# Moving four pieces of work in a fused attention and SoLU kernel: the flag's sum, one exponential, one copy, one split

## The chip, the cores and the metric

The kernel runs on one core of a Trainium2 chip. The metric is device time in microseconds (us) of one execution, the median of several runs. A core has five engines with a queue of instructions each: TensorE (PE, whose weight loads are shown as PEld), VectorE (DVE), ScalarE (ACT), GpSimd (POOL) and SyncE (SP). They run side by side and wait for each other by semaphores. Transfers are issued from the queues of SP, ACT and POOL and carried out by 16 DMA engines.

## The reference

Two stages follow each other. The first is block-sparse attention over 4 batches, 8 heads, 768 positions and 64 numbers per head; a mask of 24 by 24 blocks allows the neighbouring blocks, the first and the last row and column of blocks, and three sampled blocks for each row of blocks. The second takes the 3072 rows of 512 numbers and computes a layer with the SoLU activation and a layer norm.

```
scores = q @ k.T / sqrt(64);  scores[not mask] = -1e9
attn   = exp(scores - max) / (sum + 1e-9)
x      = (attn @ v) as rows of 8 heads x 64        # 3072 x 512
h      = x @ w_in                                  # 3072 x 1024
solu   = h * exp(h - max) / (sum + 1e-9)
ln     = (solu - mean) / sqrt(var + 1e-6) * g_ln
out    = ln @ w_out                                # 3072 x 512
```

All inputs and the output are float32 in memory; the kernel multiplies in bfloat16.

## The kernel before, in words

The work goes in 12 passes (NPASS): three for each batch, each for 256 queries (PC = 2 tiles of 128). A pass has 12 units (SLOTS): four pairs of heads (NP), three steps over the keys (UP) each. A unit is four products for the scores of two heads (`scores`, L416, tile sco, two buffers), one exponential on ScalarE over 128 x 1024 scores (`exps`, L427, tile exs), and eight products with the values (`outs`, L444, tile op). At the end of a pair DVE divides by the sums (`normalise`, L457 and L458, tile xb).

The second stage of one pass lies among the units of the next. xb is transposed to xT (by DMA, `x_turn`), `h_mms` (L487) multiplies with w_in, `e_exp` (L496) takes the exponential on ScalarE, `solu` (L508) multiplies on DVE, `ln_turn` (L513) transposes by DMA to lnT, `o_mms` (L547) multiplies with w_out, centred beforehand (w_cen), `stats` and `rstd` (L522 to L540) find the factor of the norm, `scaled` (L556, L558) applies it and `store` (L563) writes the rows.

Nothing is scheduled by a planner: `at(when, fn, ...)` puts each step at a time, counted in units, and `emit` records all steps sorted by it. What is recorded for one engine is done in that order. The changed steps are these.

- **k and q of a later batch.** They are loaded, cast by GpSimd, transposed by DMA into a tile pd and then copied by GpSimd (`shift`, shown as L327, the line of the helper `copy`) into KT and QT, since the two heads of a pair stand one below the other. For the last pair (NP - 1) q's first two of six blocks are copied ahead of k; then k whole, then q's other four.
- **e in the last pass.** In the last pass (b0 = SLOTS * LP) the layer of the pass before is squeezed into fewer units. `e_at` gives the times of e, solu and lnT of its first tile.
- **The end.** When the last attention unit is through, the last pass's own layer follows, without attention to fill the gaps. Three quarters of its xT come by DMA, the last quarter by TensorE (`x_last`, tile x_tp) and a copy on DVE (L860); `h_end` (L869) multiplies its halves, `ln_mm` and `ln_out` transpose solu over TensorE and ScalarE. In the stream of TensorE around it stand products of the layer before (o_mms of LP - 1).
- **The flag.** The kernel leaves out the maxima of both softmaxes. It therefore checks that all sums were in range: `check_r` and `check_e` write ones and zeros, `check_sum` (L930, L931) adds them up on DVE to a flag for each partition, `check_bad` (L938) adds those up with one product on TensorE, `check_out` (L941) casts it to an integer bad_i. Behind it all engines load the flag (L995) and branch (L996): only if it is not zero, a general path written as loops is run. Otherwise it is jumped over, and SP waits for all transfers (L1022).
- **The last tile's output** comes in two halves of 256 columns (`o_half`, L897, tiles oe1a and oe1b); DVE scales the first, and SP stores it (L909), ScalarE scales and stores the second (L906). The flag's product stands between the fifth and the sixth of the eight products of the second half.

Of the kernel before, what the change touches and what calls it, by code (L numbers as in the profile page):

```python
# [7 lines left out]
FP32 = mybir.dt.float32  # L8
# [200 lines left out]
def kernel(  # L209
# [11 lines left out]
    nc = tc.nc  # L221
# [13 lines left out]
    KF = d_ff // 128  # L235
# [6 lines left out]
    PC = 2  # L242
# [3 lines left out]
    NP = H // 2  # L246
# [13 lines left out]
    bad = const_pool.tile([128, 1], FP32)  # L260
    bad_i = const_pool.tile([1, 1], I32)
    ones_c = const_pool.tile([128, 1], FP32)
# [20 lines left out]
    p_sco = work.enter_context(tc.tile_pool(name="p_sco", bufs=2, space=bass.MemoryType.PSUM))  # L283
    p_op = work.enter_context(tc.tile_pool(name="p_op", bufs=1, space=bass.MemoryType.PSUM))
    p_h = work.enter_context(tc.tile_pool(name="p_h", bufs=1, space=bass.MemoryType.PSUM))
# [4 lines left out]
    def at(when, fn, *args):  # L290
        plan.append((when, len(plan), fn, args))

    def emit():
        for _, _, fn, args in sorted(plan, key=lambda x: x[:2]):
            fn(*args)
        plan.clear()
# [5 lines left out]
    def natural(b, pr, key):  # L302
        r = KR if b == 0 and key == "k" and pr else D
        if b:
            x0 = 2 * PW * pr + (PW if key == "q" else 0)
        elif key == "q":
            x0 = k_w + PW * pr
        else:
            x0 = PW + NCH * 2 * KR * (pr - 1) if pr else 0
        return nat[:, x0 : x0 + NCH * 2 * r].rearrange("p (c h r) -> p c h r", h=2, r=r)  # L310
# [84 lines left out]
    def unit(s):  # L395
        ps, r = divmod(s, SLOTS)
        pr, u = divmod(r, UP)
        b, j = divmod(ps, NPB)
        return ps, b, j, pr, u
# [174 lines left out]
    with tc.manual_schedule():  # L574
# [4 lines left out]
                          in_=bass.AP(tensor=_t32, offset=0, ap=[[2 * NR, NB], [1, 2 * NR]]))  # L579
# [59 lines left out]
        for pr in range(1, NP):  # L639
            nc.scalar.activation(  # L640
                out=natural(0, pr, "k")[:, :, :, D:KR].rearrange("p c h r -> p (c h) r"),
                in_=zer[:, 0:NB].rearrange("p (o r) -> p o r", o=1).broadcast_to(
                    [128, NCH * 2, NB]),
# [7 lines left out]
        for i, x0, x1 in ((0, 0, QW), (1, QW, S)):  # L651
            nc.tensor.matmul(m_ps[0:KR, i, 0 : x1 - x0], mask_l, sel_f[:, x0:x1],
                             start=True, stop=True)
# [4 lines left out]
        def spread(x, n):  # L658
            return x.rearrange("p (o c) -> p o c", o=1).broadcast_to([NB, n, x.shape[-1]])
# [20 lines left out]
        for h0, n, i, x0, x1 in ((0, 2, 0, 0, QW), (0, 1, 1, QW, S), (1, 1, 1, QW, S)):  # L680
            nc.scalar.copy(out=rows(QT[0], h0, h0 + n)[:, :, x0:x1],
                           in_=spread(m_ps[D:KR, i, 0 : x1 - x0], n))
# [87 lines left out]
        for s in range(n_units):  # L770
            ps, b, j, pr, u = unit(s)
# [25 lines left out]
        for b in range(1, B):  # L797
            loads, casts, turns, shifts, v_loads, v_casts = first if b == 1 else then
            t0 = SLOTS * NPB * (b - 1)
            for (key, pr), t_l, t_c in zip(kq + vs, loads + v_loads, casts + v_casts):  # L800
                at(t0 + t_l, load, nc.sync, srcs[key], b, pr, key)
                at(t0 + t_c, cast, nc.gpsimd, b, pr, key)
            for pr, t_t in enumerate(turns):
                at(t0 + t_t, turn_dma, b, pr)

            at(t0 + shifts[6] - 0.05, shift, b, NP - 1, "q", 0, PC)
            for (key, pr), t_s in zip(kq, shifts):
                at(t0 + t_s, shift, b, pr, key, PC if (key, pr) == ("q", NP - 1) else 0)


        def layer(ps, i, hs, es, os):
# [14 lines left out]
        LP = NPASS - 1  # L826
# [17 lines left out]
        for i, t0 in ((0, b0), (1, b0 + 4)):  # L844
            for when, n0, n1 in ((3.9, 0, 2), (4.85, 2, 5), (5.86, 5, 8)):
                at(t0 + when, h_mms, ps, i, n0, n1)

            e_at = (6.5, 7.0, 7.05) if i == 0 else (6.85, 6.86, 6.87)
            for when, fn in zip(e_at, (e_exp, solu, ln_turn)):
                at(t0 + when, fn, ps, i)  # L850
        at(b0 + 8.2, stats, ps, 0)
# [2 lines left out]
        def x_last():  # L854
            tp = p_op.tile([128, 1024], BF16, tag="op", name="x_tp")[:, 0 : PC * 128]
            for i in range(PC):
                nc.tensor.matmul(tp[:, i * 128 : (i + 1) * 128],
                                 xb_of[LP][:, KD - 1, i, :], ident,
                                 is_transpose=True, start=(i == 0), stop=(i == PC - 1))
            nc.vector.tensor_copy(  # L860
                out=xT_of[LP][:, (KD - 1) * PC : KD * PC, :],
                in_=tp.rearrange("p (i t) -> p i t", t=128))

# [22 lines left out]

        o2 = {}

        def o_half(half, pool, tag, c0=0, c1=KF):
            if c0:  # L890
                pass
            elif pool is p_sco:
                o2[half] = p_sco.tile([128, 2, HF], FP32, tag=tag, name="oe1a")[:, 0, 0:256]
            else:
                o2[half] = pool.tile([128, d_model], FP32, tag=tag, name="oe1b")[:, 0:256]
            for c in range(c0, c1):
                nc.tensor.matmul(o2[half], lnT_of[LP, 1][:, c, :],  # L897
                                 w_cen_sb[:, c, half * 256 : (half + 1) * 256],
                                 start=(c == 0), stop=(c == KF - 1), skip_group_check=True)
# [13 lines left out]
        def tile_in(pool, tag, name):  # L913
            if pool is p_sco:
                return lambda: p_sco.tile([128, 2, HF], FP32, tag=tag, name=name)[:, 0, :]
            return lambda: pool.tile([128, d_model], FP32, tag=tag, name=name)
# [14 lines left out]
            nc.vector.tensor_scalar(out=bad, in0=n_ok[:, 0:1], scalar1=float(n_r + n_e),  # L931
                                    scalar2=None, op0=ALU.is_lt)

        bad_ps = []

        def check_bad():
            bad_ps.append(p_h.tile([1, 1], FP32, tag="h", name="bad_ps"))
            nc.tensor.matmul(bad_ps[0], bad, ones_c, start=True, stop=True)  # L938

        def check_out():  # L940
            nc.vector.tensor_copy(out=bad_i, in_=bad_ps[0])  # L941

        end = SLOTS * NPASS
        A, V = nc.scalar, nc.vector
        for n, (fn, *args) in enumerate((
            (h_end, 0, 2, KD),
            (e_exp, LP, 0),
            (o_mms, LP - 1, 0, 5, 8),
            (scaled, LP - 1, 0, A),
            (store, LP - 1, 0),  # L950
            (stats, LP - 1, 1),
            (rstd, LP - 1, 1),
            (check_r, n_r - 2 * PC, n_r),
            (h_end, 1, 0, KD),
            (solu, LP, 0),
            (stats, LP, 0),
            (e_exp, LP, 1),
            (o_mms, LP - 1, 1, 0, 3, tile_in(p_op, "op", "o_10")),
            (ln_mm, 0),
            (ln_out, 0, A),  # L960
            (o_mms, LP - 1, 1, 3, 8),
            (solu, LP, 1),
            (rstd, LP, 0),
            (stats, LP, 1),
            (o_mms, LP, 0, 0, 2, tile_in(p_sco, "sco", "oe0")),
            (ln_mm, 1),
            (ln_out, 1, A),
            (rstd, LP, 1),
            (check_e,),
            (check_sum,),  # L970
            (o_mms, LP, 0, 2, 8),
            (scaled, LP - 1, 1, A),
            (store, LP - 1, 1),
            (scaled, LP, 0, A),
            (store, LP, 0),
            (o_half, 0, p_sco, "sco"),
            (o_half, 1, p_op, "op", 0, 5),
            (check_bad,),
            (o_half, 1, p_op, "op", 5, KF),
            (scale_half, 0, V, nc.sync),  # L980
            (check_out,),
            (scale_half, 1, A, nc.scalar),
        )):
            at(end + 0.01 * n, fn, *args)
        at(end - 5.0, x_turn, LP, 0, 2)
        at(end - 3.1, x_turn, LP, 2, KD - 1)
        at(end - 1.175, h_end, 0, 0, 2, (0,))
        at(end - 1.12, h_end, 0, 0, 2, (1,))
        at(end - 1.0, x_last)
        at(end - 1.9, check_r, 0, n_r - 2 * PC)  # L990
        at(end - 1.05, o_mms, LP - 1, 0, 0, 5)
        emit()

    work.close()
# [32 lines left out]
```

## Time and profile before

| | |
|---|---|
| time, median of 3 runs | 210.65 us (210.59 to 210.71) |
| the profiled execution | 210.66 us, of which its span is 208.9 us |
| PE busy | 198.0 us (95%) |
| ACT busy | 174.6 us (84%) |
| DVE busy | 140.3 us (67%) |
| POOL busy | 109.1 us (52%) |
| mean granted clock of TensorE | 0.991 |

The span goes from the first to the last instruction of the program; some 1.8 us lie around it. Busy times are sums over the whole span. In the timeline a row gives start, duration, engine, line, what is done, output tile and input tile with shapes and a count, and in brackets how long the engine had been idle before it and what ended that. In the waits' view a row gives who waited for whom, the sum in us, how often, and the longest. In the view of one line a row gives minimum, median and maximum in ns, and the start of the first and the last in us. In the DMA view a queue's row gives packets, MB and the packets' time as a share of the 16 engines' time in the stretch; an issue's row gives what is moved, the issuing queue, its size and the time from issue to landing.

### The profile page before, as it was taken

The page shows a single profiled execution, that of the slowest core. Times are in us where ns is not written, and L with a number is a line of the kernel's source. Part 1 is how long each engine was busy: PE and PEld are TensorE (multiplying, and loading weights), DVE is VectorE, ACT ScalarE, POOL GpSimd, SP SyncE. Part 2 cuts the span into 40 slices and gives each one's busy share as a digit, 9 for nine tenths or more (in the row PEclk, how much of TensorE's full clock was granted, in tenths as well). Part 3 has the DMA queues.
Part 4 walks back from the last instruction along what each step waited for, and adds up shares of the span by engine and source line. Part 5 has one row for each costly group of instructions (what it writes and reads, how often), then busy time and mean ns, then how long its engine had stood idle before and what let it go on. Part 6 is the DMA issues. An engine that isn't in the chain of part 4 may idle for free.

```text
span 208.9 us, 5591 instructions
## 1 busy us (share of the span) xinstructions
PE 198.0 (95%) x2204; PEld 137.9 (66%) x2238; DVE 140.3 (67%) x329; ACT 174.6 (84%) x208; POOL 109.1 (52%) x161
## 2 busy tenths in 40 slices
PE   7989999999999999999999999999999999999980
PEld 2669867676676676676666677667667667665450
DVE  5885888987656656666656656656655755768970
ACT  6898989889889889889889889888988988875750
POOL 7989698688686384377196366197450011011120
PEclk9999999999999999999999999999999999999996
DMA  5999999899999899896999899997924915635331
GB/s 159 345 364 220 369 376 275 190 199 307 154 288 277 192 252 264 201 202 169 191 323 198 195 289 236 196 284 90 250 81 89 112 54 81 163 69 84 100 123 37
DMA packets 73906, 42.02 MB, mean 201 GB/s; under 512 B 55828, under 2 KB 69396, under 8 KB 73876
## 3 DMA queue, kind: packets, MB, share of 16 engines
q1 hardware_dynamic: 72932, 40.06, 80.4%
q0 software_dynamic: 528, 1.05, 2.7%
q10 hardware_dynamic: 416, 0.52, 0.8%
q8 instruction: 18, 0.29, 0.6%
q14 instruction: 12, 0.10, 0.2%
HBM read 23.07 MB, written 6.29 MB: 141 GB/s over the span
## 4 chain that ended last, share of the span: by engine, by line
PE 81%; DMA 9%; issue 2%; POOL 2%; ACT 1%; DVE 1%; SPq 1%; POOLq 0%
PE sco L416 28%; PE o L547 17%; PE op L444 16%; PE h L487 16%; DMA st_q<-in_q_dram 3%; DMA w_out_f<-in_moe_w_out_dram 3%; DMA st_k<-in_k_dram 3%; PE he L869 1%; PE oe L547 1%; PE mean_ps L750 1%; POOL VA L327 1%; SPq L318 1%; DVE solu L508 1%; POOL nat L327 1%; ACT e L496 1%
## 5 line engine op out<-in xcount | busy, mean ns | idle before, releaser
L427 ACT ACTIVATE exs<-sco 128x1024 bf16<-128x1024 f32 x144 | 140.6, 1024 | 8.7 <-PE sco L416 6.3
L416 PE MATMUL sco<-QT,KT 88*128 88x256 bf16 x576 | 86.6, 272 | 0.8 <-ACT exs L427 0.5
L416 PEld LDWEIGHTS <-KT 88*128 88x128 bf16 x576 | 54.1, 97 | 32.4 <-issue 5.7
L444 PE MATMUL op<-VA,exs 128*128 128x65 bf16 x1152 | 51.8, 194 | 0.5
L444 PEld LDWEIGHTS <-exs 128*128 128x128 bf16 x1152 | 48.5, 97 | 3.7 <-DVE xb L458 0.3
L487 PE MATMUL h<-w_in_sb,xT 128*128 128x512 bf16 x153 | 48.6, 378 | 0.6
L547 PE MATMUL o<-w_cen_sb,lnT 128*128 128x512 bf16 x166 | 43.2, 379 | 0.5
L540 POOL TENSOR_TENSOR rstd<-vpe,mhalf 128x1 f32<-128x1 f32 x24 | 13.2, 550 | 47.8 <-DVE vpe L538 41.3
L457 DVE RECIPROCAL recip_all<-op 128x4 f32<-128x4 f32 x48 | 8.7, 182 | 41.5 <-PE op L444 41.3
L496 ACT ACTIVATE e<-h 128x1024 bf16<-128x1024 f32 x22 | 22.5, 1024 | 12.3 <-PE h L487 10.8
L522 DVE BATCH_NORM_STATS2 stats<-solu 128x6 f32<-128x512 bf16 x48 | 30.6, 679 | 0.0
L327 POOL COPY KT<-pd 64x768 bf16<-64x768 bf16 x24 | 20.1, 838 | 17.4 <-DMA pd<-nat 15.8
L508 DVE TENSOR_TENSOR solu<-h,e 128x1024 bf16<-128x1024 f32 x22 | 26.7, 1215 | 1.4 <-ACT e L496 1.3
L327 POOL COPY QT<-pd 64x768 bf16<-64x768 bf16 (+2 forms) x30 | 20.8, 694 | 10.8 <-DMA pd<-nat 9.5
L547 PEld LDWEIGHTS <-lnT 128*128 128x128 bf16 x176 | 15.9, 97 | 13.8 <-DMA lnT<-solu 0.2
L558 DVE TENSOR_SCALAR ot<-o,rstd 128x512 f32<-128x512 f32 x20 | 15.0, 750 | 10.8 <-issue 6.9
L458 DVE TENSOR_TENSOR xb<-op,recip_all 128x256 bf16<-128x256 f32 x48 | 20.4, 424 | 1.7
L487 PEld LDWEIGHTS <-xT 128*128 128x128 bf16 x176 | 16.2, 98 | 4.2 <-DMA xT<-xb 0.5
L327 POOL CAST nat<-st_q 128x768 bf16<-128x768 f32 (+2 forms) x19 | 14.0, 736 | 7.8 <-DMA st_q<-in_q_dram 7.7
L327 POOL CAST nat<-st_k 128x768 bf16<-128x768 f32 x15 | 12.7, 850 | 3.3 <-DMA st_k<-in_k_dram 3.0
L327 POOL CAST VA<-st_v 128x768 bf16<-128x768 f32 x16 | 13.4, 842 | 1.9 <-DMA st_v<-in_v_dram 1.3
L740 POOL TENSOR_SCALAR w_out_sb<-w_out_f,g_ln_sb 128x512 bf16<-128x512 f32 x8 | 5.7, 724 | 2.1 <-DMA w_out_f<-in_moe_w_out_dram 2.1
(89 smaller groups left out, 114.7 us busy)
## 6 DMA issues: line engine op xcount, KB each, us to landing
st_v<-in_v_dram SPq DMA_DIRECT2D x16, 384.0 KB, 5.2
out_dram<-ot SPq DMA_DIRECT2D x23, 256.0 KB, 2.8
st_k<-in_k_dram SPq DMA_DIRECT2D x15, 384.0 KB, 5.4
st_q<-in_q_dram SPq DMA_DIRECT2D x12, 384.0 KB, 6.9
w_out_f<-in_moe_w_out_dram SPq DMA_DIRECT2D x4, 512.0 KB, 7.5
st_q<-in_q_dram SPq DMA_DIRECT2D x4, 256.0 KB, 6.9
w_in_sb<-in_moe_w_in_dram POOLq DMA_DIRECT2D x1, 1024.0 KB, 11.5
st_q<-in_q_dram SPq DMA_DIRECT2D x4, 128.0 KB, 4.7
```

The costliest lines, as they stand in the source:

```text
L327: eng.tensor_copy(out=o, in_=i)
L416: nc.tensor.matmul(sco[:, hh, kk * QW : (kk + 1) * QW], KT[b % 2][0:KR, h * NCH + 2 * u + kk, :], QT[b % 2][0:KR, h * NCH + PC * j : h * N ...
L427: nc.scalar.activation(out=exs_of[ps, pr][:, u].rearrange("p a b c -> p (a b c)"), in_=sco_of.pop(s).rearrange("p a b -> p (a b)"), func=A ...
L444: nc.tensor.matmul(op[:, hh, ic, :], exs[:, u, hh, kk, ic * TQ : (ic + 1) * TQ], VA[b % 2][:, 2 * pr + hh, 2 * u + kk, :], start=(u == 0 a ...
L458: nc.vector.tensor_tensor(out=xb_of[ps][:, pr].rearrange("p c (h d) -> p h c d", h=2), in0=op[:, :, :, 0:D], in1=recip.broadcast_to([TQ, 2 ...
L487: nc.tensor.matmul(h_of[ps, i][:, half, :], xT_of[ps][:, c * PC + i, :], w_in_sb[:, c, half * HF : (half + 1) * HF], start=(c == 0), stop= ...
L496: nc.scalar.activation(out=o, in_=h, func=ACT.Exp, scale=1.0, accum_out=esum_all[:, t : t + 1])
L508: nc.vector.tensor_mul(out=so, in0=h, in1=e)
L522: nc.vector.bn_stats(out=stat_of[ps, i][:, half, :], in_=so[:, half, :])
L540: nc.gpsimd.tensor_tensor(out=rstd_of[ps, i], in0=vpe, in1=mhalf, op=ALU.pow)
L547: nc.tensor.matmul(ops_of[ps, i], lnT_of[ps, i][:, c, :], w_cen_sb[:, c, :], start=(c == 0), stop=(c == KF - 1), skip_group_check=True)
L558: nc.vector.tensor_scalar(out=o, in0=i_, scalar1=r, scalar2=None, op0=ALU.mult)
```

## The change

Four places are changed; the program computes the same.

- For the last pair of a later batch, k too is copied in two parts: k's first two blocks, q's first two, k's other four, q's other four.
- In the last pass, e of the first tile goes from 6.5 to 7.01 units, so that it is recorded behind the exponential at 7 and not ahead of it.
- The last quarter of x is transposed behind three of the five products of o that preceded it, and its copy to xT goes from DVE to ScalarE.
- The flag's sum on DVE goes behind the scaling of the last tile's first half, its product on TensorE behind the second half's eight products, and its cast follows.

```diff
-            at(t0 + shifts[6] - 0.05, shift, b, NP - 1, "q", 0, PC)
             for (key, pr), t_s in zip(kq, shifts):
-                at(t0 + t_s, shift, b, pr, key, PC if (key, pr) == ("q", NP - 1) else 0)
+                if pr == NP - 1:
+                    at(t0 + shifts[6] - 0.1, shift, b, pr, key, 0, PC)
+                at(t0 + t_s, shift, b, pr, key, PC if pr == NP - 1 else 0)
...
-            e_at = (6.5, 7.0, 7.05) if i == 0 else (6.85, 6.86, 6.87)
+            e_at = (7.01, 7.02, 7.05) if i == 0 else (6.85, 6.86, 6.87)
...
-            nc.vector.tensor_copy(
+            nc.scalar.copy(
                 out=xT_of[LP][:, (KD - 1) * PC : KD * PC, :],
                 in_=tp.rearrange("p (i t) -> p i t", t=128))
...
         def check_bad():
-            bad_ps.append(p_h.tile([1, 1], FP32, tag="h", name="bad_ps"))
-            nc.tensor.matmul(bad_ps[0], bad, ones_c, start=True, stop=True)
-
-        def check_out():
-            nc.vector.tensor_copy(out=bad_i, in_=bad_ps[0])
+            bad_ps = p_h.tile([1, 1], FP32, tag="h", name="bad_ps")
+            nc.tensor.matmul(bad_ps, bad, ones_c, start=True, stop=True)
+            nc.vector.tensor_copy(out=bad_i, in_=bad_ps)
...
             (check_e,),
-            (check_sum,),
             (o_mms, LP, 0, 2, 8),
...
             (o_half, 0, p_sco, "sco"),
-            (o_half, 1, p_op, "op", 0, 5),
+            (o_half, 1, p_op, "op"),
+            (scale_half, 0, V, nc.sync),
+            (check_sum,),
             (check_bad,),
-            (o_half, 1, p_op, "op", 5, KF),
-            (scale_half, 0, V, nc.sync),
-            (check_out,),
             (scale_half, 1, A, nc.scalar),
...
-        at(end - 1.05, o_mms, LP - 1, 0, 0, 5)
+        at(end - 1.05, o_mms, LP - 1, 0, 0, 3)
+        at(end - 0.95, o_mms, LP - 1, 0, 3, 5)
```

`o_half` also loses its parameters for a part of the products.

More of the change, by code (lines that the diff above doesn't have):

```diff
@@ L887, with o_half @@
         o2 = {}
[L889 to L892, printed above, removed]
+        def o_half(half, pool, tag):
+            if pool is p_sco:
                 o2[half] = p_sco.tile([128, 2, HF], FP32, tag=tag, name="oe1a")[:, 0, 0:256]
@@ L895, in o_half @@
                 o2[half] = pool.tile([128, d_model], FP32, tag=tag, name="oe1b")[:, 0:256]
-            for c in range(c0, c1):
+            for c in range(KF):
                 nc.tensor.matmul(o2[half], lnT_of[LP, 1][:, c, :],
@@ L932, in check_sum @@
                                     scalar2=None, op0=ALU.is_lt)
-        bad_ps = []
         def check_bad():
-            bad_ps.append(p_h.tile([1, 1], FP32, tag="h", name="bad_ps"))
-            nc.tensor.matmul(bad_ps[0], bad, ones_c, start=True, stop=True)
-        def check_out():
-            nc.vector.tensor_copy(out=bad_i, in_=bad_ps[0])
+            bad_ps = p_h.tile([1, 1], FP32, tag="h", name="bad_ps")
+            nc.tensor.matmul(bad_ps, bad, ones_c, start=True, stop=True)
+            nc.vector.tensor_copy(out=bad_i, in_=bad_ps)
         end = SLOTS * NPASS
```

## The prediction

> **What bounds the kernel now.** I read the page first, then the timeline of the last 33 us, then the waits of SP's queue, and last the DMA packets of the final microseconds.
>
> ```profile
> span 208.9 us, 5591 instructions
> PE 198.0 (95%) x2204; PEld 137.9 (66%) x2238; DVE 140.3 (67%) x329; ACT 174.6 (84%) x208; POOL 109.1 (52%) x161
> ```
>
> TensorE, busy 95% of the span, sets the time until its last product: anything that makes it wait in the stream is worth what it waited, anything beside it is worth nothing. After 202.8 us there is no matmul, and six microseconds of the span are still to come. That end is where most of this change lies, so I read it row by row (timeline: start, duration, engine, line).
>
> ```profile
> 200.71 1.04 PE L897 MATMUL oe1a<-w_cen_sb,lnTe 128*128 128x256 bf16 x8
> 201.28 0.38 DVE L930 TENSOR_REDUCE n_ok<-okr 128x1 f32<-128x216 f32 x1
> 201.69 0.15 DVE L931 TENSOR_SCALAR bad<-n_ok 128x1 f32<-128x1 f32 x1
> 201.84 0.48 DVE L909 TENSOR_SCALAR ot_last<-oe1a,rstd 128x256 f32<-128x256 f32 x1
> 202.22 0.19 PE L938 MATMUL bad_ps<-ones_c,bad 128*1 128x1 f32 x2
> 202.34 0.50 PE L897 MATMUL oe1b<-w_cen_sb,lnTe 128*128 128x256 bf16 x3
> 202.45 0.15 DVE L941 CAST bad_i<-bad_ps 1x1 int32<-1x1 f32 x1
> 202.93 0.47 ACT L906 ACTIVATE ot_last<-oe1b,rstd 128x256 f32<-128x256 f32 x1 [1.14 <-issue]
> 203.44 0.37 ACTq L563 DMA_DIRECT2D out_dram<-ot_last  x1
> ```
>
> The flag is summed on DVE ahead of the last scaling, TensorE multiplies it between the fifth and the sixth product of the last half, and ScalarE's scaling and store come behind the eighth. Then every sequencer loads the flag (L995), branches (L996), and SP waits for all that is outstanding (L1022). The next rows are from the views of these lines, of SP's queue waits and of the DMA issues:
>
> ```profile
> L995 SPq TENSOR_LOAD <-bad_i x1: 662/662/662, 202.7 to 202.7; - x1
> L996 SPq COMPARE_BRANCH  x1: 53/53/53, 203.8 to 203.8; - x1
> L1022 SPq EVENT_SEMAPHORE  x4: 28/28/28, 204.5 to 204.7; - x4
> SPq L1022 <- DMA out_dram<-ot_last: 2.8, 1, 2.8
> out_dram<-ot_last SPq DMA_DIRECT2D x1, 128.0 KB, 1.9
> ```
>
> SP has done its first four closing waits at 204.7 and then sits 2.8 us, to 207.5, for the last store; from there to the end it is 208.9 - 207.5 = 1.4 us. That store, issued by ScalarE at 203.44, lands 4.1 us after its issue. Its twin (the other half of the same tile, same size, issued by SP at 202.4) took 1.9. So 2.2 us of the span is a late landing. The DMA packets by queue, in the stretches 203.9 to 204.6, 204.55 to 206.1 and 206.1 to 207.2:
>
> ```profile
> q10 hardware_dynamic: 84, 0.09, 34.2%
> ...
> q10 hardware_dynamic: 67, 0.05, 15.4%
> q14 instruction: 4, 0.03, 6.8%
> q8 instruction: 1, 0.02, 4.2%
> ...
> q10 hardware_dynamic: 11, 0.01, 6.7%
> ```
>
> q10 is the store. Most of it is through by 204.6. Then five packets of instructions come (0.03 and 0.02 MB, one for each sequencer), just after the branch that jumps over the general path, and the store's last eleven packets crawl behind until 207.1. An earlier store shows the same: the view of DMA issues gives the one at 187.9, with a q8 packet inside its flight, 3.1 us, and the one at 181.2, with none, 2.2 us.
>
> ```profile
> out_dram<-ot SPq DMA_DIRECT2D x1, 256.0 KB, 3.1
> out_dram<-ot SPq DMA_DIRECT2D x1, 256.0 KB, 2.2
> ```
>
> **Last pair's k in two parts.** Of three batches only one has TensorE waiting for the last pair:
>
> ```profile
> 104.38 0.84 POOL L327 COPY QT<-pd 64x256 bf16<-64x256 bf16 x2 [4.14 <-DMA pd<-nat]
> 105.28 1.71 POOL L327 COPY KT<-pd 64x768 bf16<-64x768 bf16 x2
> 106.61 0.82 PE L416 MATMUL sco<-QT,KT 88*128 88x256 bf16 x4
> 107.99 0.60 PE L416 MATMUL sco<-QT,KT 88*128 88x256 bf16 x4
> ```
>
> The score group at 106.61 takes 0.82 instead of 0.60: its second head waits for the second k copy, done at 106.99. Afterwards GpSimd copies k's first third (0.84, to 105.2), q's (to 106.1), the rest of k (two copies of 512 columns; those of q take 1.26 in all) to 107.4, the rest of q. The group at 106.61 finds all it needs; the next, at 107.99 less 0.2, needs the rest of k, 0.4 us before it. Gain 0.2. GpSimd has two more copies, 0.84 + 1.26 - 1.71 = 0.4 us, and pushes the cast of v and one rstd behind them by that; GpSimd is busy 52% and both are used over a microsecond later. In the other two batches I count nothing. Bounds: 0 to -0.3.
>
> **e behind an exponential.**
>
> ```profile
> 182.09 0.60 PE L416 MATMUL sco<-QT,KT 88*128 88x256 bf16 x4
> 183.63 1.02 ACT L496 ACTIVATE e<-h 128x1024 bf16<-128x1024 f32 x1 [1.41 <-DVE xb L458]
> 183.87 1.68 PE L547 MATMUL o<-w_cen_sb,lnT 128*128 128x512 bf16 x7
> 185.71 0.60 PE L416 MATMUL sco<-QT,KT 88*128 88x256 bf16 x4 [0.17 <-ACT exs L427]
> ```
>
> ScalarE idles 1.41 us ahead of e, although scores written by 182.7 lie ready. Their exponential fits: 182.7 to 183.7, so e starts 0.1 late, and solu and its transposition follow 0.1 late with slack. The buffer that TensorE waits for at 185.71 is free at 183.7 instead of 185.7, and its 0.17 us (0.26 if the modelled end of the products is 0.09 late) goes. Taken: -0.2; bounds +0.1 (e's delay reaches TensorE) and -0.3.
>
> **x's last turn by ScalarE.**
>
> ```profile
> 192.41 0.28 PE L857 MATMUL x_tp<-ident,xb 128*128 128x128 bf16 x2
> 192.80 0.28 DVE L860 COPY xT<-x_tp 128x256 bf16<-128x256 bf16 x1
> 193.13 0.82 PE L869 MATMUL he<-w_in_sb,xT 128*128 128x512 bf16 x3 [0.23 <-DVE xT L860]
> 196.05 0.43 PEld L547 LDWEIGHTS <-lnT 128*128 128x128 bf16 x3 [0.22 <-DMA lnT<-solu]
> L325 ACT CAST nat<-st_k x2: 405/508/612, 4.2 to 4.8; 128x256 bf16<-128x256 f32 x1, 128x512 bf16<-128x512 f32 x1
> ```
>
> The turn moves two products of 0.22 us forward: transposed at 192.0, through at 192.3. ScalarE is idle there; its nearest copy of that size took 0.41, so xT is ready near 192.75 instead of 193.08, and h goes on 0.3 earlier. But three microseconds on, TensorE already waits 0.22 for lnT, whose transposition hangs on a solu ahead of all this, which the edit does not move. Being 0.3 earlier there makes that wait 0.5. I take 0; bounds -0.3 (lnT lands earlier too) and +0.1 (a copy of 0.7 us).
>
> **The flag behind the products.** TensorE's products of this half follow each other by 0.11 (eight in 1.04 us, the last one's tail in it). The thirteenth of the two halves starts 12 x 0.11 behind 200.71, at 202.0, so without the flag's product the next starts at 202.1, not at 202.34. Gain 0.22, straight on the path: scaling and store start 0.22 earlier. DVE scales first, at 201.8, sums at 202.2, compares 0.41 later at 202.6; TensorE's product follows at 202.8, the cast at 203.0 (0.23 behind, as now), and the flag is readable at 203.2 instead of 202.6: +0.56 for all sequencers; SP, which now loads at 202.7, +0.5. Queued behind the flag: the five loads, branches and SP's closing waits.
>
> **The sum**, against the profiled execution of 210.66 us (span 208.9, 1.76 around it; the median is 210.65). Stream: -0.2 - 0.2 + 0 = -0.4. The last store is issued at 203.44 - 0.4 - 0.22 = 202.8. Its packets began 0.5 behind the issue's end and most took 0.5, so they are through by 204.2, whereas the branch comes at 203.8 - 0.4 + 0.5 = 203.9 and the instruction packets, 0.8 us behind it now, at 204.7. The store is clear of them and lands like its twin, 1.9 us after issue: 204.7. SP's four waits end at 204.7 - 0.4 + 0.5 = 204.8. The later of the two, plus 1.4: span 206.2, time **208.0 us** (-1.3%).
>
> **Rivals.**
> - The instruction packets hold the closing code (0.14). Now the last of them ends by 206.1, 2.3 us behind SP's branch. If SP could not close before that: 203.9 + 2.3 = 206.2, 0.3 for its four waits, 1.4: span 207.9, 209.7 us. Against it: SP's four waits ran from 204.5 to 204.7, before these packets were through; what comes behind them is hidden by the store's wait. The Trainium skill, "Runtime: NRT & Kernel Launch", section "Instruction fetch mechanics", says that a taken branch to a page outside the window forces a DMA fetch of it before execution can go on; by that rule this rival holds, and the four early waits speak against it for SP at least.
> - The late landing is not the fetch's doing, or the fetch comes along 0.6 earlier (0.12): the tail stays, and the stream's 0.4 and the product's 0.22 are left: 210.0 us. For it: the last eleven packets crawl on after the instruction packets have ended. Against it: the twin's 1.9.
> - Slower (0.10): refills of instructions come with the count, not with the branch, and one falls on lnT's last transposition, on which TensorE already waits. DVE has one instruction fewer, ScalarE one more, GpSimd six. The issues of 141.4 and 193 in the DMA view:
>
> ```profile
> lnT<-solu SPq DMA_TRANSPOSE x1, 4.9
> lnT<-solu SPq DMA_TRANSPOSE x1, 3.1
> ```
>
> Then the tail stays (210.0) and 1.8 comes on top: 211.8 us. It decides once the landing passes 3.1 by more than the gains, 0.6. Against it: none of the instruction packets falls there now.
>
> **Numbers.** The forecast has 0.64: 207.3 to 208.7 by the bounds of the copies and the stream. Changes within 0.2% (0.42 us, about what a measurement of this kernel can tell from no change) come from the upper half of the second rival. Faster 0.64 + 0.14 + 0.06 = 0.84, same 0.06, slower 0.10. The range 207.2 to 210.1 leaves out the slower rival and the rest of the second.
>
> **What would show it.** Right: SP's wait for the last store is gone or under 0.3 us; that store lands under 2.2 us after issue; the instruction packets begin after its last data packet; the sco at 185.7 and 106.6 have no stall, while the wait for lnT near 195.6 has grown to some 0.5. Wrong: q10's packets still reach 2 us beyond the branch, or SP's closing waits stand in a row only after the fetch, or x's copy on ScalarE ends later than DVE's did.

## The result and the profile after

The changed kernel takes **208.11 us** (median of 5, 207.9 to 208.5), the kernel before 210.71 us beside it (5 runs, 210.59 to 211.07): ratio 0.9874, 95% interval 0.986 to 0.9888. The forecast was 208.0. (The ratios here are not the quotients of the medians beside them; the two differ by up to 0.0007.) The profiled execution took 207.95 us. Its page begins:

```profile
span 206.5 us, 5600 instructions
PE 197.8 (96%) x2204; PEld 137.3 (67%) x2238; DVE 140.2 (68%) x328; ACT 175.3 (85%) x209; POOL 110.4 (53%) x167
```

TensorE is as busy as before and the span is 2.46 us shorter. The timeline of the end (start, duration, engine, line, in brackets the idle time before and who ended it) shows where that lies:

```profile
200.59 1.04 PE L896 MATMUL oe1a<-w_cen_sb,lnTe 128*128 128x256 bf16 x8
201.46 1.04 PE L896 MATMUL oe1b<-w_cen_sb,lnTe 128*128 128x256 bf16 x8
201.72 0.48 DVE L908 TENSOR_SCALAR ot_last<-oe1a,rstd 128x256 f32<-128x256 f32 x1 [0.82 <-PE oe1a L896]
202.12 0.37 DVE L929 TENSOR_REDUCE n_ok<-okr 128x1 f32<-128x216 f32 x1
202.52 0.15 DVE L930 TENSOR_SCALAR bad<-n_ok 128x1 f32<-128x1 f32 x1
202.58 0.47 ACT L905 ACTIVATE ot_last<-oe1b,rstd 128x256 f32<-128x256 f32 x1 [0.91 <-issue]
202.82 0.19 PE L935 MATMUL bad_ps<-ones_c,bad 128*1 128x1 f32 x2 [0.32 <-DVE bad L930]
203.05 0.15 DVE L936 CAST bad_i<-bad_ps 1x1 int32<-1x1 f32 x1 [0.37 <-PE bad_ps L935]
203.09 0.37 ACTq L563 DMA_DIRECT2D out_dram<-ot_last  x1
```

The last half's eight products follow without a gap, and the flag's product comes 1.4 us behind the first of them. Counted from oe1a's first product, ScalarE's scaling starts at +1.99 (before: +2.22) and the cast of the flag at +2.46 (before: +1.74). SP's waits, and its instructions by line:

```profile
SPq L1016 <- PEq L1016: 0.7, 2, 0.5
SPq L1016 <- remote: 0.7, 1, 0.7
...
SPq L989 <- DVE bad_i L936: 0.6, 1, 0.6
```

```profile
L989 SPq TENSOR_LOAD <-bad_i x1: 471/471/471, 203.2 to 203.2; - x1
L990 SPq COMPARE_BRANCH  x1: 53/53/53, 204.1 to 204.1; - x1
L1016 SPq EVENT_SEMAPHORE  x14: 17/28/28, 204.8 to 206.4; - x14
```

The wait of 2.8 us for the last store is gone from the list. The closing waits run through from 204.8. The DMA packets by queue, first in the stretch 203 to 204.6, then from 204.6 to the end:

```profile
q1 hardware_dynamic: 213, 0.24, 41.5%
q10 hardware_dynamic: 144, 0.13, 23.4%
...
q14 instruction: 4, 0.03, 5.5%
q8 instruction: 1, 0.02, 2.7%
```

All 144 packets of the store (q10) are through by 204.6, and the five instruction packets have the time after that to themselves (the first at 204.88). By the trace's landing events the store lands 1.73 us after its issue; before it was 4.11.

What the two profiles show of the rest of the stream I read in one stretch, from the score group near 103.5 to oe1a's first product, since the time up to there differs from execution to execution even where the code is the same. That group and o's products in the last pass, before and then after:

```profile
103.46 0.60 PE L416 MATMUL sco<-QT,KT 88*128 88x256 bf16 x4
...
193.79 0.81 PE L547 MATMUL o<-w_cen_sb,lnT 128*128 128x512 bf16 x3
...
196.16 0.81 PE L547 MATMUL o<-w_cen_sb,lnT 128*128 128x512 bf16 x3
```

```profile
103.96 0.60 PE L416 MATMUL sco<-QT,KT 88*128 88x256 bf16 x4
...
107.11 0.60 PE L416 MATMUL sco<-QT,KT 88*128 88x256 bf16 x4
...
182.37 0.60 PE L416 MATMUL sco<-QT,KT 88*128 88x256 bf16 x4
185.67 0.60 PE L416 MATMUL sco<-QT,KT 88*128 88x256 bf16 x4
...
192.26 0.37 ACT L861 COPY xT<-x_tp 128x256 bf16<-128x256 bf16 x1 [1.00 <-PE x_tp L858]
193.35 0.81 PE L547 MATMUL o<-w_cen_sb,lnT 128*128 128x512 bf16 x3
196.03 0.33 PEld L547 LDWEIGHTS <-lnT 128*128 128x128 bf16 x3 [0.63 <-DMA lnT<-solu]
```

From 103.96 to 200.59 are 96.63 us; before, from 103.46 to 200.71, 97.25. So the stream is 0.62 us shorter, but this execution came to 103.5 half a microsecond later, which hides most of it: at oe1a only 0.12 is left. The group at 107.11 has no stall (0.60, before 0.82). From the score group at 182.37 to the one at 185.67 it is 3.30 us, before 3.62. The products of o behind x's turn start 0.44 earlier than before (193.35 for 193.79), and the wait for lnT has grown to 0.63.

The three parts, for all profiles of this study. "To 103" is the start of that score group, "stream" from there to oe1a's first product, "end" from there to the end of the span; "first packet" and "landing" are counted from the issue of the last store to the first instruction packet of the end, and to the store's last landing event. All in us.

| kernel | to 103 | stream | end | first packet | landing |
|---|---|---|---|---|---|
| before | 103.46 | 97.25 | 8.22 | 1.17 | 4.11 |
| after | 103.96 | 96.63 | 5.88 | 1.79 | 1.73 |
| e1_flag_only | 103.65 | 97.05 | 5.88 | 1.82 | 1.71 |
| e2_stream_only | 103.46 | 96.60 | 8.06 | 1.13 | 3.94 |
| e3_flag_cast_late | 103.18 | 97.07 | 6.72 | 2.39 | 1.71 |
| e4_sum_early | 103.61 | 96.60 | 5.72 | 1.66 | 1.72 |
| e5_no_branch | 103.22 | 97.00 | 5.44 | none | 1.71 |
| e6_ln_first | 103.56 | 96.38 | 5.62 | 1.56 | 1.72 |
| e7_flag_earliest | 103.52 | 96.64 | 7.31 | 0.38 | 3.12 |
| e8_x_only | 103.33 | 97.17 | 8.06 | 1.19 | 3.95 |
| e9_after_again | 103.40 | 96.58 | 5.90 | 1.80 | 1.72 |
| e10_sum_early_again | 103.55 | 96.62 | 5.74 | 1.71 | 1.72 |
| e11_ln_first_again | 103.72 | 96.38 | 5.65 | 1.56 | 1.71 |
| e12_k_whole | 104.45 | 96.62 | 5.75 | 1.71 | 1.72 |

"Stream" and "end" agree to some 0.07 between kernels that are alike there (where the store lands late, the end moves with its landing, by up to 0.2); "to 103" wanders over 1.3 us in kernels that do not differ there. The timed runs of one kernel are spread over about as much, so the timed medians carry the large effect and the table the small ones.

### The profile page after: what moved, and what is told of

It reads as the page before. It is cut to its first block, busy times and chain, and to the rows that moved or that the text cites. A ratio compares the mean times of both kernels' runs of the same rounds, so it can differ in the third digit from the quotient of the medians.

```text
span 206.5 us, 5600 instructions
## 1 busy us (share of the span) xinstructions
PE 197.8 (96%) x2204; PEld 137.3 (67%) x2238; DVE 140.2 (68%) x328; ACT 175.3 (85%) x209; POOL 110.4 (53%) x167
## 4 chain that ended last, share of the span: by engine, by line
PE 84%; DVE 7%; DMA 4%; POOL 2%; issue 1%; SPq 0%; DVEq 0%; POOLq 0%
PE sco L416 29%; PE op L444 18%; PE o L547 16%; PE h L487 16%; DMA st_k<-in_k_dram 2%; DMA lnT<-solu 1%; DVE stats L522 1%; DVE QT L664 1%; DVE solu L508 1%; PE oe L547 1%; PE mean_ps L750 1%; DVE KT L371 1%; POOL nat L327 1%; PE tp_k L346 1%; PE tp_q L356 1%
## 5 line engine op out<-in xcount | busy, mean ns | idle before, releaser
L327 POOL COPY KT<-pd 64x768 bf16<-64x768 bf16 (+2 forms) x30 | 21.2, 707 | 27.1 <-DMA pd<-nat 24.8
L740 POOL TENSOR_SCALAR w_out_sb<-w_out_f,g_ln_sb 128x512 bf16<-128x512 f32 x8 | 6.4, 816 | 2.9 <-DMA w_out_f<-in_moe_w_out_dram 2.9
```

Of the source, the lines that this page charges most:

```text
L327: eng.tensor_copy(out=o, in_=i)
```

## The experiments

The theory: the gain is the last store leaving the flight of the instruction packets that the branch sets off. Its rivals: the gain comes from the stream; or the late landing belongs to the store, to its queue or to the end, whatever the packets do.

**The two halves of the change.** e1 takes the flag's part alone (on the kernel before):

```
-            (check_sum,),
             (o_mms, LP, 0, 2, 8),
...
-            (o_half, 1, p_op, "op", 0, 5),
-            (check_bad,),
-            (o_half, 1, p_op, "op", 5, KF),
+            (o_half, 1, p_op, "op"),
             (scale_half, 0, V, nc.sync),
+            (check_sum,),
+            (check_bad,),
             (check_out,),
```

> The kernel before with the flag's part of the change alone. If the gain is the last store leaving the way of the instruction packets that follow the branch, nearly all of it is here: the store is issued 0.2 to 0.3 earlier (about 203.2), lands under 2.0 us after issue, all instruction packets begin after its last data packet, and the time is 208.3 to 208.6 us. If the gain comes from the stream (k, e, x), only the flag's product leaves the path: 210.4 us.

Measured: 208.32 us against 210.67, ratio 0.9888 (0.9859 to 0.9916). End 5.88, as in the changed kernel.

e2 takes the rest alone: k in two parts, e at 7.01, x by ScalarE with o's products split around it, the flag as before.

> The change without the flag's part: k in two parts, e behind an exponential, x's turn by ScalarE. By the first theory both the store and the branch come 0.1 to 0.4 earlier together, the instruction packets meet the store as before, it lands 3.5 to 4.5 us after issue: 210.3 to 210.6 us. If the stream carries the gain: 208.2 us.

Measured: 209.76 us, ratio 0.9963 (0.9942 to 0.9983). End 8.06, the store lands 3.94 after issue, SP waits 2.7 for it. That is 0.9 us, more than the 0.1 to 0.4 of the first theory and far from the 2.5 of the second; the profile has 0.65 of it in the stream and 0.16 at the end. So the flag's part carries some 2.3 us and the stream about 0.6. (The two medians add up to more than the whole change gave, 3.3 for 2.6 us; their intervals, 0.6 and 0.45 us to each side, allow it.)

**A delay that makes the kernel faster.** e3 is the kernel before with the flag's cast put on ScalarE behind everything else:

```
-            nc.vector.tensor_copy(out=bad_i, in_=bad_ps[0])
+            nc.scalar.copy(out=bad_i, in_=bad_ps[0])
...
-            (check_out,),
             (scale_half, 1, A, nc.scalar),
+            (check_out,),
```

> The kernel before with one thing moved: the cast of the flag, on ScalarE behind its last scaling and its store's issue in place of DVE. Nothing is earlier than before; the flag, and with it every branch, is about 1.5 us later (branch near 205.3, closing waits near 206.2). By the first theory this delay alone frees the store (issued 203.4, landed by 205.5, instruction packets from 206 on) and the closing row sets the end: span about 207.6, 209.4 us, faster by some 1.3 us. If the late landing belongs to the store, its queue or its place at the end and not to the instruction packets, it still lands near 207.5 and the time is 210.7 us or more.

Measured: 209.16 us, ratio 0.9924 (0.9898 to 0.995): 1.5 us faster by a later flag. The branch came at 204.6, less late than I had expected. The DMA packets in the stretches 202.9 to 204.6 and 204.6 to 207:

```profile
q1 hardware_dynamic: 164, 0.14, 24.2%
q10 hardware_dynamic: 144, 0.13, 22.1%
...
q14 instruction: 4, 0.03, 4.9%
q8 instruction: 1, 0.02, 2.7%
```

The store has the same place, the same queue and the same 0.23 us of the flag's product ahead of it as before, and lands in 1.71 instead of 4.11. That rules out the store's queue and place, and it shows that removing the product was not needed to clear the store. The loads of the flag, which move together with the branch, are not what holds the store up: in the changed kernel all five engines load between 203.2 and 204.0, inside the store's flight (203.09 to 204.81), and it lands in 1.73. Here the closing row sets the end:

```profile
L1022 SPq EVENT_SEMAPHORE  x14: 17/28/28, 205.3 to 206.9; - x14
```

**No branch.** e5 is the kernel before without these lines, so it leaves out the flag's use and the general path:

```
-    n_bad = nc.values_load(bad_i[0:1, 0:1], min_val=0, max_val=128)
-    with tc.If(n_bad > 0):
-        general_path(...)
```

> The kernel before without the flag's load, the branch and the general path behind it (that path is left out of the program; it isn't entered with these inputs). If the five instruction packets at the end are fetched because of the branch, there are none near 204.8, the last store (issued 203.4) lands 1.7 us after issue, at 205.1, and the closing row stands ready before it: span about 206.5, 208.3 us. If they come with the count of instructions, or the store lands late for another reason, it stays near 207.5 and the time near 210.

Measured: 208.45 us against 210.89, ratio 0.9882 (0.9856 to 0.9909). SP's waits, and the packets from 202.9 to 204.6:

```profile
SPq L1018 <- DMA out_dram<-ot_last: 2.3, 1, 2.3
```

```profile
q1 hardware_dynamic: 151, 0.13, 22.4%
q10 hardware_dynamic: 144, 0.13, 22.1%
```

No instruction packet comes until the closing code has run (one at 207.5, past the span of 205.7), while the 17 earlier ones of queue q8 come as before. So the five packets of the end belong to the branch, not to the count of instructions. (e5 leaves out the general path as well as the branch; that the packets follow the branch is seen in e3 and e7, where they move with it.) SP stands at the store's wait early and the end is the store's own: 5.44. The changed kernel's 5.88 is 0.44 above this, but e5 still has the flag's product ahead of the last scaling, 0.23 us that the changed kernel has not. Without it e5's end would be near 5.2, so flag, loads and branch still cost the changed kernel some 0.7 us. That is an estimate; no run has the changed order without the branch.

**The earliest flag.** e7 has the changed kernel's stream, the sum ahead, the product between the two halves, the cast ahead of the scaling:

```
+            (check_sum,),
             (o_mms, LP, 0, 2, 8),
...
             (o_half, 0, p_sco, "sco"),
+            (check_bad,),
+            (check_out,),
             (o_half, 1, p_op, "op"),
             (scale_half, 0, V, nc.sync),
-            (check_sum,),
-            (check_bad,),
```

> The changed kernel's stream with the flag as early as it can be: summed ahead, its product between the two halves, its cast ahead of DVE's scaling. The branch comes about 0.6 us earlier than in the kernel before, relative to the last store. If the end is the race of store and instruction packets, the packets are fetched from about 203.5 on, while the store's own packets wait or start, it lands 3.5 us or more after issue, and the time is 209.5 to 210.3 us: an earlier flag is worse than a later one by 2 us. If an earlier branch let the fetch pass wholly ahead of the store, it would land in under 2.5 us and the time would be 208.0 or less.

Measured: 209.36 us, ratio 0.9932 (0.9909 to 0.9954). SP's wait, the packets from 202.97 (the store's issue) to 204.3, and the branches of the five engines:

```profile
SPq L1023 <- DMA out_dram<-ot_last: 2.1, 1, 2.1
```

```profile
q10 hardware_dynamic: 121, 0.11, 25.2%
q1 hardware_dynamic: 124, 0.11, 24.0%
q14 instruction: 2, 0.02, 7.5%
q8 instruction: 1, 0.02, 6.6%
```

```profile
L997 POOLq COMPARE_BRANCH  x1: 45/45/45, 202.3 to 202.3; - x1
L997 PEldq COMPARE_BRANCH  x1: 358/358/358, 202.3 to 202.3; - x1
L997 DVEq COMPARE_BRANCH  x1: 72/72/72, 202.3 to 202.3; - x1
...
L997 SPq COMPARE_BRANCH  x1: 53/53/53, 203.3 to 203.3; - x1
L997 ACTq COMPARE_BRANCH  x1: 54/54/54, 203.9 to 203.9; - x1
```

Three instruction packets begin in this stretch, at 203.35 to 203.49; the other two follow at 204.35 and 205.01, so all five lie in the store's flight (202.97 to 206.08). It lands 3.12 after issue, a little better than I expected (3.5 or more). Three engines branch a microsecond ahead of SP here, and three packets come 1.1 us behind those three branches, one 1.1 us behind SP's and one 1.1 us behind ScalarE's. The cast is 1.2 us earlier behind oe1a than in the changed kernel (201.43 - 200.16 for 203.05 - 200.59), and the end is 1.4 us later. A third way, the fetch passing wholly ahead of the store, did not come about: ScalarE, whose queue issues the store, branches behind that issue.

**A flag a little earlier.** e4 keeps the product behind the products and puts the sum ahead again:

```
+            (check_sum,),
             (o_mms, LP, 0, 2, 8),
...
             (scale_half, 0, V, nc.sync),
-            (check_sum,),
             (check_bad,),
```

> The changed kernel with the flag summed ahead of DVE's last scaling (as in the kernel before), its product still behind all sixteen products. The flag is readable some 0.3 us earlier (cast near 202.75), and the instruction packets begin near 204.6, just behind the store's last packets (204.47 in the changed kernel). If the end is now set by flag, loads, branch and closing row, 207.8 us; if the packets catch the store again, part of the late landing returns: 208.5 to 210.0 us.

Measured: 207.44 us, ratio 0.984 (0.9811 to 0.9868). The end is 5.72 for 5.88. To compare on one chip I ran it again beside the changed kernel:

> The changed kernel as it stands, beside the next three on one chip: 208.0 to 208.3 us. Its last store is clear of the instruction packets, and in its tail the row flag, loads, branch, closing waits sets the end.

> The changed kernel with the flag summed ahead of DVE's last scaling, once more, for a comparison on one chip. The flag comes 0.4 earlier behind the products and nothing else moves: 0.3 to 0.5 us faster than the changed kernel. If the closing row does not set the end, the same as it.

Measured: 207.71 (0.9863, 0.9832 to 0.9894) and 207.5 us (0.9855, 0.9823 to 0.9886), against 210.65: not told apart by the times. (e9 lies under the 208.0 that was the least expected; its end is 5.90, as in the first profile of the changed kernel.) The flag's load, in e9 and then in e10, tells why the 0.4 us did not come through:

```profile
L989 SPq TENSOR_LOAD <-bad_i x1: 465/465/465, 202.6 to 202.6; - x1
```

```profile
L989 SPq TENSOR_LOAD <-bad_i x1: 718/718/718, 202.4 to 202.4; - x1
```

The cast is 0.39 earlier behind oe1a, but the load takes 0.72 instead of 0.47, and 0.25 is given back. The end gains 0.16 in both pairs of profiles (5.88 to 5.72, 5.90 to 5.74). What sets the length of the load stays open: it is not the start alone, since the earliest load behind oe1a (e7) took 0.48 and the latest (e3) 0.63.

**x alone.**

```
-            nc.vector.tensor_copy(
+            nc.scalar.copy(
                 out=xT_of[LP][:, (KD - 1) * PC : KD * PC, :],
...
-        at(end - 1.05, o_mms, LP - 1, 0, 0, 5)
+        at(end - 1.05, o_mms, LP - 1, 0, 0, 3)
+        at(end - 0.95, o_mms, LP - 1, 0, 3, 5)
```

> The kernel before with x's last turn copied by ScalarE alone (and its two products ahead of o's last two). By the prediction's step h starts 0.3 to 0.4 earlier and the wait for lnT takes it back: 0 to -0.1 us, 210.6. If the wait does not take it: 210.3.

Measured: 210.74 us against 210.89, ratio 0.9999 (0.9976 to 1.0023). Its timeline:

```profile
185.58 0.60 PE L416 MATMUL sco<-QT,KT 88*128 88x256 bf16 x4 [0.17 <-ACT exs L427]
...
193.26 0.81 PE L547 MATMUL o<-w_cen_sb,lnT 128*128 128x512 bf16 x3
195.94 0.82 PE L547 MATMUL o<-w_cen_sb,lnT 128*128 128x512 bf16 x3
```

From the score group to o's three products it is 7.68 us (before 193.79 - 185.71 = 8.08), to the products behind lnT 10.36 (before 196.16 - 185.71 = 10.45). So 0.40 is gained at x and 0.31 given back to lnT; 0.09 stays.

**Work in the wait for lnT.** e6 is e4 with the first solu's transposition ahead of o's products that wait for lnT, and the last reciprocals' checks behind the second solu:

```
-            (check_r, n_r - 2 * PC, n_r),
...
-            (o_mms, LP - 1, 1, 0, 3, tile_in(p_op, "op", "o_10")),
             (ln_mm, 0),
             (ln_out, 0, A),
-            (o_mms, LP - 1, 1, 3, 8),
+            (o_mms, LP - 1, 1, 0, 8, tile_in(p_op, "op", "o_10")),
             (solu, LP, 1),
+            (check_r, n_r - 2 * PC, n_r),
```

> The kernel with the early sum and the late product of the flag, and in the last pass the transposition of the first half's solu ahead of o's eight products that wait for lnT (before: behind three of them), and the two range checks of the last reciprocals behind the second solu. If x's gain of 0.39 us at h is eaten by the wait for lnT, as its trace shows (0.30 of it given back at 195.65), other work in that wait gets part of it back: solu 0.2 earlier, ScalarE's copy of ln_tp 0.25 earlier, oe's first products 0.25 earlier: 207.2 us against 207.44. If the wait is only shown there and something else is late, no change: 207.4 to 207.5.

> The same, with the transposition of the first solu ahead of o's products in the wait for lnT, and two checks later. Its trace had the last halves 0.27 earlier than without: 0.25 us faster than the run with the early sum alone. If the time does not follow the trace's stream, the same as that run.

Measured: e6 207.85 us (ratio 0.9856, 0.9835 to 0.9877), over the 207.2 expected; e11, on the chip of e10, has the ratio 0.985 (0.9814 to 0.9886) beside e10's 0.9855. Both profiles have the stream at 96.38, 0.24 under e10's; the times do not show it. The mechanism is there, the gain is smaller than what the runs resolve. No version beats the changed kernel by a measured time; by the profiles e6's is the shortest (stream and end 102.0 us, the changed kernel's 102.5).

**k whole.** e12 is e10 with k copied whole:

```
-            for (key, pr), t_s in zip(kq, shifts):
-                if pr == NP - 1:
-                    at(t0 + shifts[6] - 0.1, shift, b, pr, key, 0, PC)
-                at(t0 + t_s, shift, b, pr, key, PC if pr == NP - 1 else 0)
+            at(t0 + shifts[6] - 0.05, shift, b, NP - 1, "q", 0, PC)
+            for (key, pr), t_s in zip(kq, shifts):
+                at(t0 + t_s, shift, b, pr, key, PC if (key, pr) == ("q", NP - 1) else 0)
```

> The run with the early sum, its last pair's k copied whole as in the kernel before. By the prediction's step the score group near 106.6 stalls 0.2 us again in every execution: 0.2 us slower. By what the traces since show, it stalls only where an instruction packet at 101 lies in the flight of the pair's transposition (pd landing 4.7 us after issue), and not where that packet comes near 98 (3.1 us): 0 to 0.2 us slower, by the execution.

Measured: 207.93 us, ratio 0.9868 (0.9837 to 0.9899), 0.43 above e10, with intervals that overlap; its profile has the same stream, 96.62, and no stall at that score group. The difference of its profile lies ahead, in "to 103". What decides whether k whole costs its 0.2 is seen in the kernels that have it: before and e8 stall, e1, e3, e5 and e12 don't. The pair's transposition and the instruction packet ahead of it, by the DMA view of before (100.5 to 101.8):

```profile
q8 instruction: 1, 0.02, 4.6%
...
pd<-nat SPq DMA_TRANSPOSE x1, 5.0
```

and of e1 (97.5 to 99, then 99.2 to 100.2), with the copy and the score group from its timeline:

```profile
q8 instruction: 1, 0.02, 4.0%
...
pd<-nat SPq DMA_TRANSPOSE x1, 3.2
```

```profile
102.86 0.84 POOL L327 COPY QT<-pd 64x256 bf16<-64x256 bf16 x2 [2.43 <-DMA pd<-nat]
...
106.81 0.60 PE L416 MATMUL sco<-QT,KT 88*128 88x256 bf16 x4
```

The ninth packet of q8 comes at 101.0 in the one and at 98.1 in the other. With the packet in its flight the transposition takes 5.0 us, with the packet ahead of it 3.2; GpSimd then starts 1.5 us earlier (102.86 for 104.38) and the whole k is in time. In e3, e5, e10, e11 and e12 the packet came at 97.4 to 99.1 and the transposition took 3.2 to 3.4, in e2, e4, e6, e7, e8, e9 and after it came at 100.8 to 101.5 and the transposition took 5.0. The two go together in all 14 profiles; that the packet is the cause was not tested by moving it alone. Why it comes at one or the other is open: both are seen in the same program, e4 and e10.

## Why the prediction was right

- **The store leaves the instruction packets.** Right by its steps, and shown: later flag alone (e3) and no branch (e5) both bring the landing to 1.71. With the first packet 1.56 us or more after the issue the store lands in 1.7, with it 0.4 to 1.2 after in 3.1 to 4.1. The forecast put the end behind oe1a at 206.2 - 200.3 = 5.9; it is 5.88. One figure of this step holds less widely than it was used: the first packet 0.8 us behind SP's branch. It is 0.82 in after, but 0.09 in e7. What all profiles share is 1.1 us behind the first branch of any engine (1.09 to 1.18), and in before and after that branch is GpSimd's, 0.3 ahead of SP's.
- **What then sets the end.** The prediction had the landing and the end of SP's four waits 0.1 apart, 204.7 and 204.8. The store takes 1.73, not 1.9, and is down at 204.81; the four waits end at 205.06, and the wait for the store behind them, at 205.09, takes no time. So flag, load, branch and closing waits set the end, as e4 and e10 confirm (an earlier flag, a shorter end, with the store issued 2.50 behind oe1a in all of them).
- **The flag's product, -0.22.** Measured -0.23 at ScalarE's scaling.
- **The flag's delay, +0.56.** The cast is 0.72 later behind oe1a (forecast 0.55 for it), mostly since TensorE's product starts 0.30 behind the comparison's start, where I put 0.2. SP's branch is only 0.41 later, because its load took 0.47 instead of 0.66. Two errors of opposite sign.
- **e behind an exponential, -0.2.** Mis-sized: -0.32, just past the bound of -0.3. The bracket showed a stall of 0.17, but a group's duration has the modelled tail of its last product in it, and the prediction put only 0.09 for that. Products of o follow each other by 0.217 (seven took 1.68, three 0.81: a quarter of the difference), so the seven from 183.87 leave the next start at 185.39, and it came at 185.71. The stall was 0.32, and start to start shows it: 3.62 from the score group at 182.09 to the one at 185.71, and 3.62 in e1, e3, e5 and e8 too, where e is as before, against 3.30 in after.
- **x by ScalarE, 0.** Right: 0.37 for the copy (0.41 was put), 0.40 at h, given back to lnT but for 0.09.
- **k in two parts, -0.2.** True of the execution that I read, and zero in others: of the whole-k profiles two stall and four don't. The step took one execution's landing of a transposition as the kernel's.
- **The sum.** Stream -0.62 in place of -0.4, and yet the total is right to 0.1. The profiled execution of after reached the score group of 103.5 half a microsecond late, so its span is 206.5 where 206.2 was forecast, and 1.5 us lie around its span where the sum had 1.76. That these cancel is luck; the end's -2.34 (forecast -2.3) is not.
- **The rivals.** Packets that hold the closing code: no. In after every engine has gone on behind its branch by 204.82 (SP's first closing wait, the last of the five), ahead of the first packet at 204.88, and the last packet is still under way when the span ends. The Trainium skill, "Runtime: NRT & Kernel Launch", section "Instruction fetch mechanics", says that a taken branch out of the window forces a fetch before execution goes on. The fetch is there (e5 has none), a halt until it lands is not; whether the code behind the branch lies out of the window no view tells. A late landing that is not the fetch's doing: no, by e3 and e5. The slower rival, a refill on lnT's last transposition: no packet fell there, but a delay of that size is seen where one falls on a transposition, pd's 5.0 against 3.2.

## What to carry to other kernels

When a store at the end lands late, look in the DMA view for instruction packets in its flight: a flag that is ready early may send the branch, and the code behind it, into the last transfer, and delaying it can be the faster order. Read a stall from start to start, not from the bracket alone, and read a small term from more than one execution before it goes into a sum. Split the span at fixed instructions (here three parts): it tells gains of a tenth of a microsecond where the whole time wanders by one.

## What the runs showed of the hardware

- Five instruction packets (48 KB in all) beside a store of 128 KB cost it 1.4 to 2.4 us (landing at 3.12 in e7, 3.94 in e2, 3.95 in e8 and 4.11 in before, against 1.71), though in before they themselves take 0.3 to 1.0 us each. Thirteen of the store's sixteen landing events come at 1.6 to 1.8 us in before, as in an undisturbed one, and three at 2.7, 3.3 and 4.1: a part of it is held up, and its last eleven packets go on slowly after the fetch has ended (the last instruction packet ends at 206.0, the store's last packet at 207.1). The Trainium skill, "DMA: Bandwidth & Descriptors", section "Queues, rings and completion order", says that each DMA engine takes turns between the rows that it has work for; that would fit a store of which only a part is late, but no view here names the engine of a packet, and the slow end behind the fetch is not explained by it.
- An engine's instruction packet comes 1.07 us or more behind that engine's own branch, mostly 1.1, and its next instruction 0.4 to 0.9 us behind the branch, so ahead of the packet. This holds in all 13 profiles with a branch (which packet of q14 is whose is inferred from their order).
- SP's load of the flag took 0.47 us in after and e9, 0.66 in before and 0.72 in e10; SP's first closing wait stands 0.7 to 0.9 us behind its branch (0.5 in e7).
- The refills of a straight stream come about every 11 us on q8 (9 to 13 us apart from 25 to 188 us of before), and one of them moved by 3 us between two executions of one program (101.1 in e4, 97.7 in e10). Between the kernels with the whole k, a move of that size goes with a stall of 0.22 or none.
